# The second block's second product by a seven-product scheme, in passes of 768 tokens

## The chip, the cores and the metric

One core of one Trainium2 chip runs the whole program. The metric is the device time of one execution in microseconds. Before the change it is 907.19 us, the median of 3 runs (907.12 to 916.56).

## The reference, cut to what matters

```
attn_out = local band attention + upsampled attention on 4-token means   # q, k, v: 4 x 8 x 576 x 64
x  = attn_out as 2304 tokens x 512
h1 = x @ w_in        # 512 -> 2048
g1 = h1 * (1 / (1 + exp(-1.702 * h1)))
y  = g1 @ w_out      # 2048 -> 512
h2 = y @ w_in2       # second block, same sizes
g2 = maximum(0.01 * h2, h2)
out = g2 @ w_out2    # the product that the change recasts
```

The weights arrive as float64 bits; 512 KB hold one 128x512 tile of them.

## The kernel before

Everything is kept transposed: features lie on the 128 partitions, tokens along the columns. Each matrix product is made of three TensorE products, since every operand is split into a high part (rounded to the fp32r format) and a low part (the rest): low by high, high by low, high by high. One matmul has a 128x128 weight tile and a moving tile of up to 512 token columns.

A block is cut into token passes (`TB1` = 512, 448, 448, 448, 448 for the first block, `TB2` = 512, 512, 512, 512, 256 for the second). A unit is one pass j with one of 16 slices m of the 2048 hidden features: `l1_part` (line 723) makes 12 matmuls into an h bank (4 slices kc of 128 input features, 3 products each), `gate` (line 740) makes the activation and its two parts (ScalarE, VectorE, ScalarE, GpSimd: lines 753 or 760, 754 or 761, 151, 765), and `l2` (line 770) makes 12 matmuls into four output banks that collect over all 16 m. `l2` runs two units behind `l1_part` (`LAG` = 2). After the last m the four banks are scaled and stored, for the first block to the DRAM tensors `yd`, for the second to the output (lines 787 to 793).

Each engine works through its instructions in the order of the program text (`manual_schedule`, line 839). The attention and the first 14 units follow a list written out by hand (`ORDER`); from unit 14 on a loop (lines 853 to 873) runs `l1_part`, `gate`, the attention turns that are left, `l2`, and then weight work. All transfers are issued from SyncE's one queue.

The second block's weights are made while the first block runs. Between units 38 and 65 `w_next` (line 209) turns one float64 tile into float32 (`w_bits`, lines 160 to 183: one copy, three VectorE operations) and stores it to `wd`. During the first block's last pass `w_back` (line 226) reads both float32 tiles of an m back and splits them (ScalarE line 235, GpSimd line 236) into one of 16 weight slots of 8 KB per partition, in which they stay for the rest of the kernel.

Of the kernel before, what the change touches and what calls it, by code (L numbers as in the profile page):

```python
# [7 lines left out]
F32 = mybir.dt.float32  # L8
F32R = mybir.dt.float32r
# [7 lines left out]
P = 128  # L17
# [10 lines left out]
def attn_moe_kernel(ctx: ExitStack, tc, qT_d, kT_d, vh_d, vg_d, w1a, w2a, w1b, w2b, outT):  # L28
# [71 lines left out]
    ap = ctx.enter_context(tc.tile_pool(name="ap", bufs=1))  # L100
# [6 lines left out]
    wd = [dram.tile([P, 2, DM], F32, name=f"wd_{m}") for m in range(NM)]  # L107


    warm = const.tile([P, P], BF16, name="warm")  # L110
# [35 lines left out]
    def on(default):  # L146
        return chosen[0] or default
# [58 lines left out]
    pos = [0, 0]  # L206
    made = []

    def w_next():

        if made:
            m, i, t = made.pop()
            nc.sync.dma_start(out=wd[m][:, i], in_=t)
        while pos[0] < min(len(w_order), pos[1] + 3):
            w_load(1, *w_order[pos[0]])
            pos[0] += 1
        if pos[1] < len(w_order):
            m, i = w_order[pos[1]]
            t, fs = w_bits(1, m, i)
            run(fs)  # L220
            made.append((m, i, t))
        pos[1] += 1

    back = {}

    def w_back(m):

        while len(back) < min(NM, m + 3):
            n = len(back)
            back[n] = cv.tile([P, DM], I64, tag="stage", name=f"b_{n}", bufs=3).bitcast(F32)  # L230
            nc.sync.dma_start(out=back[n].rearrange("p (i n) -> p i n", n=DM), in_=wd[n])
        w_slot(1, m)
        t = back[m].rearrange("p (i n) -> p i n", n=DM)
        w = wt[1, m].rearrange("p (i k) n -> p i k n", k=2)
        nc.scalar.activation(out=w[:, :, 0].bitcast(F32R), in_=t, func=AF.Copy)  # L235
        nc.gpsimd.tensor_tensor(out=w[:, :, 1].bitcast(F32R), in0=t, in1=w[:, :, 0], op=ALU.subtract)  # L236

    ND, DS, DN = 3, 40, 48
# [437 lines left out]


    blk = []
    for e, tb in ((0, TB1), (1, TB2)):
        t0 = 0
        for n in tb:
            blk.append((e, t0, n))
            t0 += n
        assert t0 == NT
    units = [(j, m) for j in range(len(blk)) for m in range(NM)]
    NB1 = len(TB1)
    TM = max(TB1 + TB2)  # L690
    xs = {}

    def load_x(j, kc):
        e, t0, n = blk[j]
        t = mp.tile([P, TM], F32, tag="xf", name=f"xf_{j}_{kc}", bufs=KC)
        if e == 0:
            a = t0
            while a < t0 + n:
                b, o = divmod(a, S)
                w = min(S - o, t0 + n - a)  # L700
                nc.sync.dma_start(out=t[:, a - t0 : a - t0 + w], in_=xd[b][kc][:, o : o + w])
                assert jobs[NP * b + kc].done == S
                a += w
        else:
            nc.sync.dma_start(out=t[:, :n], in_=yd[kc][:, t0 : t0 + n])
        xf[j, kc] = t

    def split_hi(j, kc):
        n = blk[j][2]
        hi = mp.tile([P, TM], F32R, tag=f"xh{kc}", name=f"xh_{j}_{kc}")[:, :n]  # L710
        lo = mp.tile([P, TM], F32R, tag=f"xl{kc}", name=f"xl_{j}_{kc}")[:, :n]
        xs[kc] = (hi, lo)
        copy(hi, xf[j, kc][:, :n])

    def split_lo(j, kc):
        hi, lo = xs[kc]
        f = xf.pop((j, kc))[:, : blk[j][2]]
        on(V if j >= NB1 else XLO[kc]).tensor_tensor(out=lo, in0=f, in1=hi.bitcast(F32), op=ALU.subtract)  # L718

    gs = {}  # L720
    hs = {}

    def l1_part(u, kcs, bank=None):
        j, m = u
        w1h, w1l = wt[blk[j][0], m, 0]
# [6 lines left out]
        h = hs[u][:, : blk[j][2]]  # L732
        for kc in kcs:
            for i, (w, part) in enumerate(((w1l, 0), (w1h, 1), (w1h, 0))):
                nc.tensor.matmul(  # L735
                    h, w[:, kc * P : (kc + 1) * P], xs[kc][part],
                    start=kc == 0 and i == 0, stop=kc == KC - 1 and i == 2,
                )

    def gate(u):  # L740

        j, m = u
        n = blk[j][2]
# [6 lines left out]
        if blk[j][0] == 0:  # L750

            fs = [
                lambda: nc.scalar.activation(out=g, in_=h[:, :n], func=AF.Tanh, scale=0.5 * 1.702),  # L753
                lambda: nc.vector.scalar_tensor_tensor(  # L754
                    out=g, in0=g, scalar=1.0, in1=h[:, :n], op0=ALU.add, op1=ALU.mult
                ),
            ]
        else:
            fs = [
                lambda: nc.scalar.activation(out=g, in_=h[:, :n], func=AF.Copy, scale=0.01),  # L760
                lambda: nc.vector.tensor_tensor(out=g, in0=g, in1=h[:, :n], op=ALU.max),  # L761
            ]
# [6 lines left out]

    def l2(u):  # L770
        j, m = u
        e, t0, n = blk[j]
        gh, gl = gs.pop(u)
        w2h, w2l = wt[e, m, 1]
# [10 lines left out]
        scale = 0.5 if e == 0 else 1.0  # L785
        dst = yd if e == 0 else [outT[c * P : (c + 1) * P, :] for c in range(KC)]
        for c in range(KC):
            y = mp.tile([P, TM], F32, tag="xf", name=f"y_{j}_{c}", bufs=KC)[:, :n]
            if c % 2:
                nc.scalar.activation(out=y, in_=acc[c][:, :n], func=AF.Copy, scale=scale)  # L790
            else:
                nc.vector.tensor_scalar(out=y, in0=acc[c][:, :n], scalar1=scale, scalar2=None, op0=ALU.mult)
            nc.sync.dma_start(out=dst[c][:, t0 : t0 + n], in_=y)

    TURN, PERIOD = 2 * UNITS - 4, 6
    XL = NM - 4
# [42 lines left out]
    with tc.manual_schedule(engines={ET.PE, ET.DVE, ET.Pool, ET.Activation, ET.SP}):  # L839
# [10 lines left out]
            token(name)  # L850
        chosen[0] = None

        for u in range(UNITS, len(units) + LAG):
            if u < len(units):
                j, m = units[u]
                l1_part(units[u], range(KC))
                if m == NM - 1 and j + 1 < len(blk):
                    for kc in range(KC):
                        split_hi(j + 1, kc)
                        split_lo(j + 1, kc)  # L860
                run(gate(units[u]))
            run(turns.get(2 * u, []))
            if u >= LAG:
                l2(units[u - LAG])
                if units[u - LAG][0] == NB1 - 1:
                    w_back(units[u - LAG][1])
            while pos[1] < min(len(w_order) + 1, (u - AHEAD[0]) * len(w_order) // (AHEAD[1] - AHEAD[0])):
                w_next()
            run(turns.get(2 * u + 1, []))
            if u < len(units) and j + 1 < len(blk):  # L870
                for kc in range(KC):
                    if j > 1 and m == XL:
                        load_x(j + 1, kc)


# [47 lines left out]
```

## Time and profile before

| | us |
|---|---|
| median of 3 runs | 907.19 |
| the profiled execution's own time | 907.32 |
| its span, first to last instruction | 905.5 |
| PE busy in it | 895.1 |
| DVE, ACT, POOL busy | 405.7, 323.8, 337.7 |

PE is TensorE's matmuls, PEld its weight loads, DVE VectorE, ACT ScalarE, POOL GpSimd, SP SyncE (SPq its queue). Matmuls overlap one another, so the duration shown for one (0.39 us at 512 columns) is longer than the distance to the next; the rate is read from the starts, or from the pieces of the chain of waits, which gives a run of matmuls with its count. Attention and the first block's early units fill the first 300 us, the first block alone runs to about 503 us, the second block from there to the end.

### The profile page before, as it was taken

What the parts mean: (1) busy time and instruction counts of PE and PEld (TensorE: products, weight loads), DVE (VectorE), ACT (ScalarE), POOL (GpSimd) and SP (SyncE); (2) the same over time, 40 slices, a digit from 0 to 9 for tenths busy, and PEclk for the clock granted to TensorE, in tenths of its full rate; (3) what the DMA queues carried; (4) which work ended last, traced back from release to release, by engine and by line L of the source; (5) the groups of instructions that cost most, each with busy time, mean ns of one, the idle gap of its engine ahead of it and who ended that gap; (6) DMA issues with size and microseconds to landing.
All of it is one profiled execution on the core that took longest, in us unless ns stands there. A gap on an engine that the chain in (4) does not pass through costs nothing.

```text
span 905.5 us, 14436 instructions
## 1 busy us (share of the span) xinstructions
PE 895.1 (99%) x5681; PEld 764.4 (84%) x5681; DVE 405.7 (45%) x723; ACT 323.8 (36%) x713; POOL 337.7 (37%) x322
## 2 busy tenths in 40 slices
PE   8999999999999999999999999999999999999998
PEld 4687877888888899999999888888888888888898
DVE  7979997644455489888411311211121112111211
ACT  6865565322253123223344522322232223222322
POOL 5543535543554324224477622222222222222221
PEclk9999999999999999999999999999999999999999
DMA  8835543555444656666644300020002000200000
GB/s 279 273 111 157 187 163 108 167 151 144 152 131 133 204 177 224 230 198 227 195 136 142 132 1 1 1 93 1 1 1 93 1 1 1 70 0 1 29 20 24
DMA packets 51908, 98.70 MB, mean 109 GB/s; under 512 B 11648, under 2 KB 22912, under 8 KB 51840
## 3 DMA queue, kind: packets, MB, share of 16 engines
q1 hardware_dynamic: 51840, 97.77, 33.9%
q8 instruction: 45, 0.74, 0.3%
q14 instruction: 23, 0.19, 0.1%
HBM read 72.97 MB, written 24.77 MB: 108 GB/s over the span
## 4 chain that ended last, share of the span: by engine, by line
PE 96%; DVE 2%; ACT 1%; DMA 1%; issue 0%; SPq 0%; ACTq 0%
PE acc L780 44%; PE h L735 44%; PE av L568 2%; PE avd L509 2%; PE sc L351 1%; PE scd L434 1%; DMA a<-qT 1%; PE pt L528 0%; ACT a L407 0%; DVE a L325 0%; PE pdt L461 0%; DVE stat L402 0%; DVE stat_d L441 0%; DVE t L175 0%; DVE t L179 0%; DVE stat L398 0%
## 5 line engine op out<-in xcount | busy, mean ns | idle before, releaser
L780 PE MATMUL acc<-gh,w 128*128 128x512 f32 (+2 forms) x1280 | 393.5, 371 | 0.0
L735 PE MATMUL h<-xh,w 128*128 128x512 f32 (+2 forms) x1280 | 392.8, 370 | 0.0
L765 POOL TENSOR_TENSOR gl<-g,gh 128x512 fp32r<-128x512 f32 (+2 forms) x149 | 176.0, 1181 | 443.4 <-ACT gh L151 431.7
L780 PEld LDWEIGHTS acc<-gh,w 128*128 128x128 f32 x1280 | 237.3, 188 | 35.1 <-issue 2.0
L735 PEld LDWEIGHTS h<-xh,w 128*128 128x128 f32 x1280 | 237.3, 188 | 33.2
L735 PE MATMUL h<-xl,w 128*128 128x512 f32 (+2 forms) x640 | 236.2, 369 | 0.0
L780 PE MATMUL acc<-gl,w 128*128 128x512 f32 (+2 forms) x640 | 236.1, 369 | 0.0
L761 DVE TENSOR_TENSOR g<-g,h 128x512 f32<-128x512 f32 (+1 forms) x80 | 50.7, 634 | 315.5 <-ACT g L760 315.5
L151 ACT ACTIVATE gh<-g 128x512 fp32r<-128x512 f32 (+2 forms) x160 | 94.3, 590 | 123.5 <-DVE g L754 66.9
L735 PEld LDWEIGHTS h<-xl,w 128*128 128x128 f32 x640 | 120.5, 188 | 16.1
L780 PEld LDWEIGHTS acc<-gl,w 128*128 128x128 f32 x640 | 120.4, 188 | 15.7
L760 ACT ACTIVATE g<-h 128x512 f32<-128x512 f32 (+1 forms) x80 | 44.4, 555 | 220.9 <-PE h L735 220.6
L754 DVE SCALAR_TENSOR_TENSOR g<-g,h 128x448 f32<-128x448 f32 (+1 forms) x80 | 50.5, 632 | 122.9 <-ACT g L753 122.4
L753 ACT ACTIVATE g<-h 128x448 f32<-128x448 f32 (+1 forms) x80 | 44.3, 554 | 166.5 <-PE h L735 158.9
L175 DVE SCALAR_TENSOR_TENSOR t<-s,t 128x512 uint32<-128x512 uint32 x64 | 63.9, 1003 | 1.5
L198 POOL TENSOR_TENSOR w<-t,w 128x512 fp32r<-128x512 f32 x25 | 33.7, 1354 | 51.6 <-ACT w L151 46.5
L179 DVE SCALAR_TENSOR_TENSOR t<-s,t 128x512 uint32<-128x512 uint32 x64 | 45.6, 718 | 1.5
L236 POOL TENSOR_TENSOR w<-b,w 128x1024 fp32r<-128x1024 f32 x16 | 38.4, 2401 | 8.1 <-ACT w L235 8.1
L378 POOL TENSOR_TENSOR P<-P,stat 128x320 f32<-128x320 f32 (+1 forms) x37 | 30.0, 828 | 29.2 <-DVE stat L417 24.5
L172 DVE TENSOR_SCALAR t<-t 128x512 uint32<-128x512 uint32 x64 | 30.8, 484 | 3.5 <-ACT t L151 2.3
L718 DVE TENSOR_TENSOR xl<-xf,xh 128x512 fp32r<-128x512 f32 (+2 forms) x27 | 20.1, 760 | 17.6 <-ACT xh L151 17.6
L151 ACT ACTIVATE xh<-xf 128x512 fp32r<-128x512 f32 (+2 forms) x40 | 23.3, 589 | 12.5 <-PE h L735 10.3
(97 smaller groups left out, 561.9 us busy)
## 6 DMA issues: line engine op xcount, KB each, us to landing
s<-w1a SPq DMA_DIRECT2D x16, 512.0 KB, 4.2
s<-w2a SPq DMA_DIRECT2D x16, 512.0 KB, 4.1
s<-w1b SPq DMA_DIRECT2D x16, 512.0 KB, 3.9
s<-w2b SPq DMA_DIRECT2D x16, 512.0 KB, 4.3
wd<-t SPq DMA_DIRECT2D x32, 256.0 KB, 2.5
b<-wd SPq DMA_DIRECT2D x16, 512.0 KB, 3.6
xf<-yd SPq DMA_DIRECT2D x16, 256.0 KB, 3.6
outT<-y SPq DMA_DIRECT2D x16, 256.0 KB, 2.2
```

The lines of the kernel that those rows point to most:

```text
L151: return nc.scalar.activation(out=out, in_=in_, func=AF.Copy, scale=scale)
L175: lambda: nc.vector.scalar_tensor_tensor(out=b, in0=bits[:, :, 1], scalar=0x80000000, in1=b, op0=ALU.bitwise_and, op1=ALU.bitwise_or,),
L179: lambda: nc.vector.scalar_tensor_tensor(out=b, in0=bits[:, :, 0], scalar=29, in1=b, op0=ALU.logical_shift_right, op1=ALU.bitwise_or,),
L198: lambda: on(G).tensor_tensor(out=lo, in0=t, in1=wt[e, m][:, 2 * i, :], op=ALU.subtract),
L236: nc.gpsimd.tensor_tensor(out=w[:, :, 1].bitcast(F32R), in0=t, in1=w[:, :, 0], op=ALU.subtract)
L735: nc.tensor.matmul(h, w[:, kc * P : (kc + 1) * P], xs[kc][part], start=kc == 0 and i == 0, stop=kc == KC - 1 and i == 2,)
L753: lambda: nc.scalar.activation(out=g, in_=h[:, :n], func=AF.Tanh, scale=0.5 * 1.702),
L754: lambda: nc.vector.scalar_tensor_tensor(out=g, in0=g, scalar=1.0, in1=h[:, :n], op0=ALU.add, op1=ALU.mult),
L760: lambda: nc.scalar.activation(out=g, in_=h[:, :n], func=AF.Copy, scale=0.01),
L761: lambda: nc.vector.tensor_tensor(out=g, in0=g, in1=h[:, :n], op=ALU.max),
L765: lambda: on(G).tensor_tensor(out=gl, in0=g, in1=gh.bitcast(F32), op=ALU.subtract),
L780: nc.tensor.matmul(acc[c][:, :n], w[:, cs], g, start=m == 0 and i == 0, stop=m == NM - 1 and i == 2)
```

## The change

`TB2`, `w_next` and `w_back` go, and `gate` and `l2` serve the first block only. A class `Second` computes the second block in three passes p of 768 tokens, each two halves j of N2 = 384. Its first product is the same 12 matmuls per slice and half. Its second product is taken as a 2x2 by 2x2 block product: the 2048 hidden features in two halves k of 8 slices q, the 512 output features in two halves of 256, the tokens in two halves of 384. Seven block products of sums and differences take the place of eight. VectorE makes the sums on the activation side (four subtractions per q), the products go to four banks in two pairs, and the results are put together in SBUF as they are evicted.

Weights: during the first block (units 43 to 75, the list `prep`, spread evenly by weights noted in it, none in the unit with m = 14) the float64 tiles are converted with the copy on ScalarE, the four sums per q are made on VectorE, all is split, and the parts are stored to DRAM: `ws1` (16 x 512 KB) and `ws2` (8 x 1792 KB). In the second block nothing stays: per pass 16 tiles of `ws1` (512 KB) and 14 tiles of `ws2` (1 MB: four q of one product) are read, each two tiles ahead of use. The weight slots then hold 40 raw activations, a ring of five split operands, the `ws2` tiles and the next pass's input.

The order in the second block: 16 groups (p, q, k, j) of 12 matmuls fill the first chunk (four q); then each of six chunks takes 28 steps of 6 matmuls (7 products x 4 q), between which the 16 groups of the next chunk are laid; the last chunk has none. `prepare` makes the split operand three steps ahead.

```diff
-    TB2 = [512, 512, 512, 512, 256]
+    N2 = 384
+    NPAIR = NT // (2 * N2)
...
-    AHEAD = (38, 65)
+    PREP = (42, 75)
...
+    def prep_sums(q, k):
...
+        nc.vector.tensor_tensor(out=sm[:, k], in0=x, in1=y, op=op)
+    def split(hi, lo, t, e=None):
+        copy(hi.bitcast(F32R), t)
+        (e or G).tensor_tensor(out=lo.bitcast(F32R), in0=t, in1=hi, op=ALU.subtract)
...
+    def prep_store(q):
+        nc.sync.dma_start(out=ws2[q // QC][:, :, q % QC], in_=made.pop(("o", q)))
...
+    for q in range(NQD):
+        conv = [(w, lambda k=k: prep_conv(k)) for k, w in enumerate((0.3, 0.5, 1.0, 0.7))]
+        sums = [(0.4, lambda q=q, k=k: prep_sums(q, k)) for k in range(4)]
+        part = [(0.3, lambda q=q, k=k: prep_split(q, k)) for k in range(4)]
...
+        prep += conv + last + conv + sums + part[:2] + conv + low + part[2:] + conv[:3] + slow + store + conv[3:] + high
+        last = shigh
...
+    class Second:
...
+        SEQ = ((0, B11, 0, 0), (3, T1, 1, 0), (1, B21, 0, 1), (6, B22, 1, 1), (5, B12, 0, 0), (4, T2, 1, 0), (2, T4, 0, 1))
...
+        def first(self, p, q, k, j):
+            m = q + NQD * k
+            if j == 0:
+                self.load_w1()
...
+            pool, tag = ((ps_h, "h"), (ps_t, "t"))[self.n_h % 2]
...
+            for kc in range(KC):
+                hi, lo = self.x[p, j, kc]
+                ks = slice(kc * P, (kc + 1) * P)
+                for i, (a, x) in enumerate(((1, hi), (0, lo), (0, hi))):
+                    nc.tensor.matmul(
+                        h, w[:, a, ks], x, start=kc == 0 and i == 0, stop=kc == KC - 1 and i == 2
+                    )
+            g = self.free.pop(0)
+            nc.scalar.activation(out=g, in_=h, func=AF.Copy, scale=0.01)
+            nc.vector.tensor_tensor(out=g, in0=g, in1=h, op=ALU.max)
...
+            for o, a, b in ((t1, r[1], r[0]), (t2, r[3], t1), (r[1], r[3], r[1]), (t4, r[2], t2)):
+                nc.vector.tensor_tensor(out=o, in0=a, in1=b, op=ALU.subtract)
...
+        def prepare(self):
...
+            nc.scalar.activation(out=hi, in_=t, func=AF.Copy)
+            nc.gpsimd.tensor_tensor(out=lo, in0=t, in1=hi.bitcast(F32), op=ALU.subtract)
...
+        def products(self, ch, i, qs, cts):
...
+                    for k, (a, g) in enumerate(((1, hi), (0, lo), (0, hi))):
+                        nc.tensor.matmul(
+                            self.bank[pair, ct][:, :N2], w[:, q, a, cs], g,
...
+        def evict(self, ch, i, ct):
...
+            if c == 0 and i not in (4, 5):
+                nc.scalar.activation(out=y[name], in_=ps, func=AF.Copy)
+            else:
+                nc.vector.tensor_tensor(out=y[name], in0=ps, in1=y[name], op=ALU.add)
...
+            elif i == 5:
+                for n, half, j in (("e46", 1, 1), ("e7", 0, 1), ("e5", None, 0)):
+                    nc.vector.tensor_tensor(out=y[n], in0=y["u2"], in1=y[n], op=ALU.add)
...
+            elif i == 6:
+                store(y["e5"], 1, 0)
+        def second(self, s):
+            ch, i, q = self.steps[s]
+            if q == 0:
+                self.load_w2()
+            last = s >= len(self.steps) - QC
+            while self.n_prep < min(len(self.steps), s + 1 + (QC if last else self.LOOK)):
+                self.prepare()
...
+                for n in range(per):
+                    self.second(ch * per + n)
+                    while gs2 and len(gs2) > 16 - (n + 1) * 16 / 25:
+                        self.first(*gs2.pop(0))
...
+            if u > PREP[0] and m != NM - 2:
+                part = (u - PREP[0]) / (PREP[1] - PREP[0]) * sum(w for w, _ in prep)
+                while done < len(prep) and sum(w for w, _ in prep[: done + 1]) < part + 0.1:
+                    prep[done][1]()
```

## Rows read from the trace of the kernel before

**Rows 1.** The page, part 1: busy us, share of the span, instructions of each engine.

```profile
PE 895.1 (99%) x5681; PEld 764.4 (84%) x5681; DVE 405.7 (45%) x723; ACT 323.8 (36%) x713; POOL 337.7 (37%) x322
```

**Rows 2.** The page, part 4: chain that ended last, by engine.

```profile
PE 96%; DVE 2%; ACT 1%; DMA 1%; issue 0%; SPq 0%; ACTq 0%
```

**Rows 3.** Windows: us, engines' busy us, granted clock, DMA share, GB/s.

```profile
320.00:480.00 160.00, 160.00 (x791) 148.31 (x790) 108.72 (x156) 52.62 (x87) 66.53 (x48) 1.00 0.60 197
0.00:50.00 50.00, 43.51 (x569) 28.85 (x570) 42.10 (x99) 35.88 (x148) 28.14 (x38) 1.00 0.80 257
```

**Rows 4.** Chain of waits, pass of 512 columns: start us, us, what.

```profile
543.21 2.72 PE acc L780 x12
```

**Rows 5.** Chain of waits, pass of 448 columns, first and last of five pieces.

```profile
490.78 2.44 PE acc L780 x12
...
500.51 2.43 PE acc L780 x12
```

**Rows 6.** Chain of waits, last pass (256 columns) and end.

```profile
893.49 1.44 PE h L735 x12
...
897.81 4.33 PE acc L780 x36
...
902.16 0.38 ACT y L790
```

**Rows 7.** Timeline, the stores of the output at the end.

```profile
901.54 1.79 SPq L793 DMA_DIRECT2D outT<-y  x4
```

**Rows 8.** Groups by shape, second block (512 to 906 us): count, busy us, mean ns.

```profile
L761 DVE TENSOR_TENSOR g<-g,h 128x512 f32<-128x512 f32 x63 | 43.3, 687 | 272.4 <-ACT g L760 272.3
L718 DVE TENSOR_TENSOR xl<-xf,xh 128x512 fp32r<-128x512 f32 x12 | 8.2, 693 | 8.1 <-ACT xh L151 8.1
L761 DVE TENSOR_TENSOR g<-g,h 128x256 f32<-128x256 f32 x16 | 6.7, 421 | 40.6 <-ACT g L760 40.6
...
L718 DVE TENSOR_TENSOR xl<-xf,xh 128x256 fp32r<-128x256 f32 x4 | 1.7, 425 | 3.2 <-ACT xh L151 3.2
...
L765 POOL TENSOR_TENSOR gl<-g,gh 128x512 fp32r<-128x512 f32 x63 | 81.7, 1296 | 254.5 <-ACT gh L151 254.5
L765 POOL TENSOR_TENSOR gl<-g,gh 128x256 fp32r<-128x256 f32 x16 | 11.8, 736 | 36.7 <-ACT gh L151 33.2 <-PE acc L780 3.4
...
L151 ACT ACTIVATE gh<-g 128x512 fp32r<-128x512 f32 x63 | 39.9, 633 | 47.8 <-DVE g L761 47.8
...
L151 ACT ACTIVATE gh<-g 128x256 fp32r<-128x256 f32 x16 | 6.7, 417 | 7.8 <-DVE g L761 7.8
```

**Rows 9.** Groups by shape, first block alone (320 to 480 us).

```profile
L765 POOL TENSOR_TENSOR gl<-g,gh 128x448 fp32r<-128x448 f32 x33 | 38.4, 1164 | 87.9 <-ACT gh L151 80.2 <-PE acc L780 5.0 <-DMA wd<-t 2.7
L175 DVE SCALAR_TENSOR_TENSOR t<-s,t 128x512 uint32<-128x512 uint32 x29 | 38.2, 1316 | 1.0
...
L179 DVE SCALAR_TENSOR_TENSOR t<-s,t 128x512 uint32<-128x512 uint32 x30 | 20.8, 692 | 1.0
...
L172 DVE TENSOR_SCALAR t<-t 128x512 uint32<-128x512 uint32 x29 | 14.1, 485 | 1.0
```

**Rows 10.** Timeline, GpSimd and VectorE at once: start us, us, engine, instruction.

```profile
311.25 0.42 DVE L152 TENSOR_SCALAR t<-s 128x512 f32<-128x512 f32 x1
311.29 1.39 POOL L765 TENSOR_TENSOR gl<-g,gh 128x448 fp32r<-128x448 f32 x1 [4.81 <-ACT gh L151]
...
385.76 1.16 POOL L765 TENSOR_TENSOR gl<-g,gh 128x448 fp32r<-128x448 f32 x1 [3.71 <-ACT gh L151]
385.90 1.57 DVE L175 SCALAR_TENSOR_TENSOR t<-s,t 128x512 uint32<-128x512 uint32 x1
```

**Rows 11.** Timeline, one unit's gate, its first and last instruction.

```profile
481.15 0.55 ACT L753 ACTIVATE g<-h 128x448 f32<-128x448 f32 x1 [1.43 <-PE h L735]
...
483.04 1.16 POOL L765 TENSOR_TENSOR gl<-g,gh 128x448 fp32r<-128x448 f32 x1 [0.85 <-ACT gh L151]
```

**Rows 12.** The page, part 6: a read of split weights, KB, us to landing.

```profile
b<-wd SPq DMA_DIRECT2D x16, 512.0 KB, 3.6
```

More of the change, by code (lines that the diff above doesn't have):

```diff
@@ L106, in attn_moe_kernel @@
     yd = [dram.tile([P, NT], F32, name=f"yd_{c}") for c in range(KC)]
-    wd = [dram.tile([P, 2, DM], F32, name=f"wd_{m}") for m in range(NM)]
+    NQD = NM // 2
+    QC = 4
+    ws1 = [dram.tile([P, 2 * DM], F32, name=f"ws1_{m}") for m in range(NM)]
+    ws2 = [dram.tile([P, 7, QC, 2, DM // 2], F32, name=f"ws2_{c}") for c in range(NQD // QC)]
     warm = const.tile([P, P], BF16, name="warm")
@@ L205, in attn_moe_kernel @@
     w_order = [(m, i) for m in range(NM) for i in range(2)]
[L206 to L236, printed above, removed]
+    prep_order = [(m, i) for q in range(NQD) for i in (1, 0) for m in (q, q + NQD)]
@@ new lines, in attn_moe_kernel, with prep_conv @@
+    at = {"load": 0, "conv": 0}
+    made = {}
+    def prep_conv(k):
+        if k == 0:
+            while at["load"] < min(len(prep_order), at["conv"] + 3):
+                w_load(1, *prep_order[at["load"]])
+                at["load"] += 1
+            m, i = prep_order[at["conv"]]
+            at["conv"] += 1
+            made[m, i], made["fs"] = w_bits(1, m, i)
+            chosen[0] = nc.scalar
+        made["fs"][k]()
+        chosen[0] = None
+    def prep_sums(q, k):
+        H = DM // 2
+        t0, t1 = made[q, 1], made[q + NQD, 1]
+        if k == 0:
+            made["s", q] = rp.tile([P, 4, H], F32, tag="rs", name=f"sm_{q}")
+            made["o", q] = rp.tile([P, 7, 2, H], F32, tag="ra", name=f"wo_{q}")
+        sm = made["s", q]
+        x, y, op = (
+            (t0[:, H:], t1[:, H:], ALU.add),
+            (sm[:, 0], t0[:, :H], ALU.subtract),
+            (t0[:, :H], t0[:, H:], ALU.subtract),
+            (t1[:, :H], sm[:, 1], ALU.subtract),
+        )[k]
+        nc.vector.tensor_tensor(out=sm[:, k], in0=x, in1=y, op=op)
@@ new lines, in split, with prep_split @@
+    def split(hi, lo, t, e=None):
+        copy(hi.bitcast(F32R), t)
+        (e or G).tensor_tensor(out=lo.bitcast(F32R), in0=t, in1=hi, op=ALU.subtract)
+    def prep_split(q, k):
+        H = DM // 2
+        wo = made["o", q]
+        if k == 0:
+            split(wo[:, 0, 0], wo[:, 0, 1], made.pop((q, 1))[:, :H])
+        elif k == 1:
+            t = made.pop((q + NQD, 1)).rearrange("p (a n) -> p a n", n=H)
+            split(wo[:, 1:3, 0], wo[:, 1:3, 1], t)
+        else:
+            a = 2 * k - 4
+            split(wo[:, 3 + a : 5 + a, 0], wo[:, 3 + a : 5 + a, 1], made["s", q][:, a : a + 2])
@@ new lines, in prep_store, with prep_first, prep_store_first @@
+    def prep_store(q):
+        nc.sync.dma_start(out=ws2[q // QC][:, :, q % QC], in_=made.pop(("o", q)))
+    def prep_first(m):
+        t = made.pop((m, 0))
+        o = rp.tile([P, DM], F32, tag="rw", name=f"w1o_{m}", bufs=2)
+        split(o, t, t)
+        made["f", m] = (o, t)
+    def prep_store_first(m):
+        for i, t in enumerate(made.pop(("f", m))):
+            nc.sync.dma_start(out=ws1[m][:, i * DM : (i + 1) * DM], in_=t)
+    prep = []
+    last = []
+    for q in range(NQD):
+        conv = [(w, lambda k=k: prep_conv(k)) for k, w in enumerate((0.3, 0.5, 1.0, 0.7))]
+        sums = [(0.4, lambda q=q, k=k: prep_sums(q, k)) for k in range(4)]
+        part = [(0.3, lambda q=q, k=k: prep_split(q, k)) for k in range(4)]
+        low, high = [[(0.3, lambda m=m: prep_first(m))] for m in (q, q + NQD)]
+        slow, shigh = [[(0.0, lambda m=m: prep_store_first(m))] for m in (q, q + NQD)]
+        store = [(0.0, lambda q=q: prep_store(q))]
+        prep += conv + last + conv + sums + part[:2] + conv + low + part[2:] + conv[:3] + slow + store + conv[3:] + high
+        last = shigh
@@ L241, in attn_moe_kernel @@
+    prep += last
     ND, DS, DN = 3, 40, 48
@@ L681, in attn_moe_kernel @@
     blk = []
[L682 to L687, printed above, removed]
+    t0 = 0
+    for n in TB1:
+        blk.append((t0, n))
+        t0 += n
+    assert t0 == NT
     units = [(j, m) for j in range(len(blk)) for m in range(NM)]
-    NB1 = len(TB1)
-    TM = max(TB1 + TB2)
     xs = {}
     def load_x(j, kc):
-        e, t0, n = blk[j]
+        t0, n = blk[j]
         t = mp.tile([P, TM], F32, tag="xf", name=f"xf_{j}_{kc}", bufs=KC)
[L696 to L705, printed above, removed]
+        a = t0
+        while a < t0 + n:
+            b, o = divmod(a, S)
+            w = min(S - o, t0 + n - a)
+            nc.sync.dma_start(out=t[:, a - t0 : a - t0 + w], in_=xd[b][kc][:, o : o + w])
+            assert jobs[NP * b + kc].done == S
+            a += w
         xf[j, kc] = t
     def split_hi(j, kc):
-        n = blk[j][2]
+        n = blk[j][1]
         hi = mp.tile([P, TM], F32R, tag=f"xh{kc}", name=f"xh_{j}_{kc}")[:, :n]
@@ L795, in attn_moe_kernel @@
+    sec = Second()
     TURN, PERIOD = 2 * UNITS - 4, 6
@@ L851, in attn_moe_kernel @@
         chosen[0] = None
[L853 to L858, printed above, removed]
+        done = 0
+        rp = None
+        for u in range(UNITS, len(units)):
+            j, m = units[u]
+            l1_part(units[u], range(KC))
+            if m == NM - 1:
+                for kc in range(KC):
+                    if j + 1 < len(blk):
                         split_hi(j + 1, kc)
                         split_lo(j + 1, kc)
-                run(gate(units[u]))
+                    else:
+                        sec.split_x(0, 0, kc)
+            run(gate(units[u]))
             run(turns.get(2 * u, []))
[L863 to L868, printed above, removed]
+            l2(units[u - LAG])
+            if u > PREP[0] and m != NM - 2:
+                part = (u - PREP[0]) / (PREP[1] - PREP[0]) * sum(w for w, _ in prep)
+                while done < len(prep) and sum(w for w, _ in prep[: done + 1]) < part + 0.1:
+                    prep[done][1]()
+                    done += 1
             run(turns.get(2 * u + 1, []))
-            if u < len(units) and j + 1 < len(blk):
+            if u == PREP[0]:
+                ap_open.__exit__(None, None, None)
+                rp = ctx.enter_context(tc.tile_pool(name="rp", bufs=1))
+            if j + 1 < len(blk):
                 for kc in range(KC):
@@ L873, in attn_moe_kernel @@
                         load_x(j + 1, kc)
+            else:
+                if m == 2:
+                    for kc in range(KC):
+                        sec.load_raw(0, 1, kc)
+                if 6 <= m < 6 + KC:
+                    sec.split_x(0, 1, m - 6)
+                if m == 10:
+                    for kc in range(KC):
+                        sec.load_raw(0, 0, kc)
+                if m == 13:
+                    for _ in range(2):
+                        sec.load_w1()
+        assert done == len(prep)
+        sec.free = [x for k in range(8) for x in sec.cut(f"raw_{k}", F32)]
+        for _ in range(2):
+            sec.load_w2()
+        sec.main([lambda u=u: l2(units[u]) for u in range(len(units) - LAG, len(units))])
 def kernel(q, k, v, moe_w_in, moe_w_out, moe2_w_in, moe2_w_out):
```

193 lines of the change are left out of this document (168 added, 25 removed).

## The prediction

> **What bounds the kernel now.** I read the busy shares first: PE is busy for 895.1 of 905.5 us, no other engine for half of the span [rows 1]. Busy time alone proves nothing for overlapping matmuls, so the chain of waits comes next: 96% of it is PE, and neither a queue nor "issue" has a share [rows 2]. In the second block the chain is an unbroken row of pieces of 12 matmuls. What counts is the distance between starts: 2.72 us for 12 at 512 columns, 226.7 ns each [rows 4]; 1.44 us at 256 columns, 120.0 ns each [rows 6]; and from 490.78 to 500.51 us four pieces at 448 columns, 2.43 us each, 202.7 ns a matmul [rows 5]. Two units of any stretch cost the same, so no wait reaches PE there. The granted clock is 1.00 (2.4 GHz) throughout, also where the DMA engines are busy at 0.60 and 0.80 [rows 3]. PE's work is the time; the question is what the change takes from it and whether the new side work stays hidden.
>
> **PE's work.** In the second block there are 4 passes x 16 units x 24 = 1536 matmuls of 512 columns and 384 of 256. At the distances above that is 348.2 + 46.1 = 394.2 us. After the change the first product has 6 halves x 16 slices x 12 = 1152 matmuls of 384 columns, the second 3 passes x 7 products x 8 q x 2 output tiles x 3 = 1008, together 2160 (eight products would make 2304). No row has 384 columns in fp32r. It lies midway between 256 and 512, whose distances fit one line: (120.0 + 226.7) / 2 = 173.3 ns. The other end is the row at 448 columns: at 2.4 GHz these take 186.7 ns, the row shows 202.7, so 16.0 on top, against 13.3 at 256 and 512; with 16.0, 384 columns cost 176.0 ns. I take 173.3, since two rows that enclose 384 agree on it. 2160 x 173.3 = 374.4 us: **19.8 us less**. With 176.0 it is 380.2 us, 14.1 less. So the eighth saved of one product is partly paid back by 240 more matmuls of fixed cost.
>
> The Trainium skill (TensorE: Matmul & The Clock Gate, "Wait — 56ns, not 53.3ns?") puts the distance at N / 2.4 GHz plus about 2.5 ns. By that, an estimate, the block would go from 373.4 to 351.0 us, a gain of 22.4. It was measured in bf16; the fp32r rows here show 13.3 on top, and they decide.
>
> **Side work in the second block.** One chunk has 28 steps x 6 and 16 groups x 12 matmuls, (168 + 192) x 173.3 ns = 62.4 us of PE. Prices at 384 columns, midway between the rows at 256 and 512: VectorE from PSUM 554 ns, from SBUF 559, GpSimd 1016, ScalarE 525 [rows 8]. GpSimd: 28 low parts, 28.4 us. ScalarE: 16 + 28 copies, at most 10 evictions and 8 input splits, 32.6 us. VectorE: 16 maxima, 16 sums, 14 additions at eviction, 8 input splits, 30.0 us. Each is about half of 62.4, and there are four h banks in place of two, three steps of lead (3.1 us, 5 or more with the groups between) for a split that takes 0.53 + 1.02 us, and at least four steps between the eviction of a pair of banks and its next use. I cost it at nothing; PE's 62.4 us per chunk are the cover. The cover is thinnest in the last chunk, which has no groups: a step takes PE 1.04 us and GpSimd 1.02. Four of its 28 operands are made ahead, so GpSimd has 24.4 us of work in 24.9. It holds, and if each step took GpSimd 0.1 us more, the 2.4 us of lateness would be met by the ring's lead of four steps less one split, 4.16 - 1.55 = 2.6 us.
>
> Transfers there: 48 weight tiles of 512 KB, 42 of 1 MB, 4.7 MB in and 4.7 out, 78.6 MB in 374 us, 210 GB/s; in the last chunk 1 MB per 4.16 us, 252 GB/s. The opening 50 us moved 257 at a share of 0.80 [rows 3]. A 512 KB read lands in 3.6 us [rows 12]; a 1 MB read, with no row, in between that and twice it, 7.2 us, while two tiles of lead are 8.3 us in the last chunk and 19 elsewhere. On SyncE's queue a tile load waits for the buffer that PE frees just before, and an output store for VectorE's addition; behind such a store stand only loads that still have a tile's time. No cost, 3 us as upper end.
>
> **The first block's side work.** PE's work before 503 us is unchanged. The preparation moves from units 38 to 65 and the last pass into units 43 to 75: 33 units x 24 x 202.7 ns = 160.5 us. What hides it is the lag of two units: from the end of `l1_part` to the same unit's `l2` lie four pieces of 2.43 us, 9.7 us, and the gate needs 481.15 to 484.20, 3.1 us [rows 11]. So 6.6 us of lateness are free.
>
> Two resources come near their limit. First GpSimd and VectorE together, which hinder each other: with the GpSimd operation begun at 385.76 us, VectorE's next one lasted 1.57 us in place of 0.69, ending 0.55 after GpSimd's; with VectorE's begun at 311.25, GpSimd's lasted 1.39 in place of 1.16, ending 1.01 after [rows 9, 10]. They take turns, and only about 0.15 us of each operation lies outside its turn. GpSimd after the change: 33 gates x 1.164, 8 x (0.736 + 3 x 1.296) of splits, 16 x 1.296, 6 input splits x 1.164, 103 us. VectorE: 64 x 0.692 and 32 x 0.485 of conversion, 32 sums of 256 columns x 0.425, and 3.6 of input splits, 77 us. Laid end to end, 180 us; less 0.15 for each of the 221 operations, 147 us, 92% of 160.5. Second the DMA engines: 16.8 MB of float64, 8.4 + 14.7 MB of stores, 5.2 MB of x and y, 45.1 MB, 281 GB/s. Rows 3 give 328 (197 / 0.60) or 321 (257 / 0.80) at a share of 1, so 0.86 to 0.88. Both fit, but with cross-waits between queues: a split on ScalarE waits for VectorE's sums, and the next gate is queued behind it; a copy there waits for a float64 tile, which can stand behind a 1.8 MB store, 5.6 us at 325 GB/s. The unit with m = 14 gives no preparation and the next twice as much. I take **1 us** of stalls, between 0 and 8, near 0 because 6.6 us of slack take such bursts one by one. Dropping `w_back` (GpSimd and ScalarE, hidden) gains nothing.
>
> **The end.** Before, the last eviction ends 0.4 us after PE's last matmul [rows 6] and the stores follow [rows 7]. After, the evictions of product i = 5 put 8 additions on VectorE, 4.5 us, beside 4.16 us of PE; then two more of 0.55 come, 5.6 us, so the last ends 1.4 us after PE: **1 us more**, between 0.3 and 1.3 (192 KB to store for 128).
>
> **Sum.** Profiled execution 907.3 - 19.8 + 1 + 1 = **889.5 us**; that execution lies 0.1 us above the median, which changes nothing.
>
> **The rivals.** *A matmul of 384 columns costs 16.0 ns on top.* For it: the row at 448; against it: 256 and 512 agree on 13.3. Then 907.3 - 14.1 + 2 = 895 us.
>
> *GpSimd and VectorE become the bound of units 43 to 75.* If the turns were whole operations, 180 us stand against 160.5, 20 late; 6.6 are absorbed, so 13 to 20 us of PE stalls in place of 1: 902 to 908 us, no gain. For it: the 1.57 us of rows 10. Against it: the overlap of 0.15 in the same rows, 147 us; it decides only if waits between the queues leave the pair unused for over 8% of the time. The Trainium skill (SBUF — State Buffer, "Who interferes with whom") has this as a rule: a VectorE operation with two SBUF inputs, or in a two-port mode, and a GpSimd operation that reads SBUF exclude each other for the whole instruction. That they exclude each other the trace shows; for the whole of it, it does not.
>
> *The DMA engines become the bound there: slower.* If the queue, with 2 KB rows written to DRAM between the reads, could give no more than the 197 GB/s that the weight preparation moves now [rows 3] in place of 281, 45.1 MB would need 229 us, 68 late and 6.6 of it absorbed, some 950 us. It is slower by 1% once it delivers under about 240 (188 us for the stretch). For it: no row shows 281. Against it: 257 in the opening at a share of 0.80, and 197 at only 0.60.
>
> That it makes fewer products than eight is read from the loops, so I give no chance to the change not being what it says.
>
> **Chances and range.** A measurement here tells 1% (898.1 to 916.3 is no change). Forecast 0.58, near 889.5, with its bounds 886.5 to 894. 384 columns dearer, 0.12: 895. The pair as bound, 0.14: mostly no change, 0.02 of it below 898. DMA as bound, 0.09: slower. Left over 0.07, several late transfers or operands in the last chunks, 892 to 898, 0.01 of it slower. Faster 0.58 + 0.12 + 0.02 + 0.06 = 0.78, same 0.12, slower 0.10. The range 886.5 to 899 holds the forecast, the dearer matmul and the leftovers, about 0.78: its low end is the forecast without stalls and with the least tail and another 1 us of PE's distance, its high end the stalls of 8 us with half the dearer distance.
>
> **What would show it.** Matmuls of 384 columns 173.3 ns apart (the first step), 12 in 2.08 us; 2160 of them. PE's pieces of 2.43 us unbroken between 330 and 490 us, with VectorE's conversions longer than 0.69 us beside GpSimd's low parts (the preparation). A share of DMA below 0.9 there. After PE's last matmul some 1.4 us of VectorE. It would be wrong if PE shows gaps on GpSimd's low part in the last chunk, or on a weight tile.

## The result: no gain, 24 us lost before the second block begins

| | us |
|---|---|
| before, median of 20 runs | 907.56 |
| changed kernel, median of 20 runs | 914.84 (lowest 912.66) |
| ratio, 95% interval | 1.0085 (1.0065 to 1.0105) |
| forecast | 889.5, range 886.5 to 899 |

The profiled execution of the changed kernel took 923.17 us, span 921.4; unlike most of the 20 (by its time and mean clock only the one of 923.80 is like it) it runs 20 us of the opening at a granted clock of 0.50 (1.2 GHz), which costs 9.0 us (a run of first-block matmuls that starts at 156.69 us before starts at 165.68 here) and is taken off below.

The page of the changed kernel, parts 1 and 4 (beside [rows 1, 2]; the chain in part 4 reaches back to 416 us only, so its shares add up to some 54%):

```profile
PE 894.1 (97%) x5921; PEld 814.0 (88%) x5921; DVE 536.9 (58%) x901; ACT 383.8 (42%) x905; POOL 455.2 (49%) x442
...
PE 41%; DVE 7%; DMA 2%; ACT 2%; issue 2%; SPq 0%; DVEq 0%; ACTq 0%
```

The chain of waits, 96% PE before, now passes through DVE, ACT and DMA. Where it does so, the windows show (us, busy us of PE, PEld, DVE, ACT, POOL, granted clock, DMA share, GB/s):

```profile
40.00:60.00 20.00, 20.00 (x164) 16.20 (x161) 7.97 (x23) 7.83 (x31) 9.53 (x9) 0.50 0.37 103
...
355.00:535.00 180.00, 165.37 (x771) 146.97 (x770) 129.36 (x161) 82.09 (x155) 108.21 (x83) 0.97 0.70 241
549.00:914.00 365.00, 363.86 (x2098) 363.27 (x2097) 174.43 (x269) 137.63 (x307) 183.52 (x168) 1.00 0.56 200
```

From 549 us on PE is full. From 355 to 535 us, in the weight preparation, it is not, although no other engine is busy for more than 72% there. The chain gives the size of the loss (start us, us, what):

```profile
531.11 2.48 PE h L776 x12
533.59 2.48 PE acc L814 x12
536.07 4.17 PE h L908 x24
```

The second block's first product starts at 536.07, where the kernel before had it at 502.94 [rows 5, the piece after the last]: 33.1 us later, 9.0 of it from the opening, **24.1 us from the preparation**. Below, "lateness" is this figure for each kernel, read from its trace in the same way, at the last matmul of 448 columns before the second block and less what the opening gave; a further wait as the second block begins is not in it.

Not all of the 24.1 us are waits. Counted from start to start of the matmuls, 16.5 us lie at eleven gaps (PE's idle time in them is 14.6), 4.4 us in some 10 us at a granted clock of 0.50, 1.2 GHz (442.3 to 449.1 and 524.2 to 527.7 us, each beginning inside or between such gaps; matmuls of 448 columns start some 370 ns apart there, for 203), and 3.3 us in the slower rhythm of the last section.

From the second block's start to PE's last matmul at 917.1 us it is 381 us: the forecast's 374.4, 5.0 for the two `l2` of the first block that follow, and some 1.5, nearly all of it at one late weight tile.

### The profile page after: what moved, and what is told of

Its sections match the earlier page's. It is cut to its first block, busy times and chain, and to the rows that moved or that the text cites. A ratio compares the mean times of both kernels' runs of the same rounds, so it can differ in the third digit from the quotient of the medians.

```text
span 921.4 us, 15797 instructions
## 1 busy us (share of the span) xinstructions
PE 894.1 (97%) x5921; PEld 814.0 (88%) x5921; DVE 536.9 (58%) x901; ACT 383.8 (42%) x905; POOL 455.2 (49%) x442
## 4 chain that ended last, share of the span: by engine, by line
PE 41%; DVE 7%; DMA 2%; ACT 2%; issue 2%; SPq 0%; DVEq 0%; ACTq 0%
PE h L908 21%; PE p L955 18%; DVE t L181 2%; DVE t L185 1%; DVE t L178 1%; PE acc L814 1%; DVE sm L243 1%; DMA v<-ws 1%; DVE g L793 1%; ACT t L157 1%; PE h L776 1%; DMA s<-w1b 1%; ACT wo L157 1%; DMA s<-w2b 0%; DVE y L987 0%
## 5 line engine op out<-in xcount | busy, mean ns | idle before, releaser
L934 POOL TENSOR_TENSOR ring<-raw,ring 128x384 fp32r<-128x384 f32 x168 | 183.7, 1114 | 193.4 <-ACT ring L933 193.1
L776 PE MATMUL h<-xh,w 128*128 128x448 f32 (+1 forms) x640 | 203.7, 380 | 9.3 <-DVE g L793 8.8
L814 PE MATMUL acc<-gh,w 128*128 128x448 f32 (+1 forms) x640 | 201.8, 377 | 3.3 <-ACT gh L157 3.3
L955 PE MATMUL p<-ring,v 128*128 128x384 f32 x1008 | 188.0, 334 | 0.0
L955 PEld LDWEIGHTS p<-ring,v 128*128 128x128 f32 x1008 | 175.8, 188 | 0.3 <-POOL ring L934 0.3
L799 POOL TENSOR_TENSOR gl<-g,gh 128x448 fp32r<-128x448 f32 (+1 forms) x69 | 87.3, 1265 | 130.2 <-ACT gh L157 127.9
L776 PEld LDWEIGHTS h<-xh,w 128*128 128x128 f32 x640 | 122.2, 191 | 26.7 <-DVE g L793 11.7
L814 PEld LDWEIGHTS acc<-gh,w 128*128 128x128 f32 x640 | 121.0, 189 | 19.8 <-ACT gh L157 4.0
L776 PE MATMUL h<-xl,w 128*128 128x448 f32 (+1 forms) x320 | 120.7, 377 | 1.9 <-POOL xl L759 1.9
L814 PE MATMUL acc<-gl,w 128*128 128x448 f32 (+1 forms) x320 | 119.3, 373 | 0.1
L792 ACT ACTIVATE g<-h 128x448 f32<-128x448 f32 (+1 forms) x80 | 44.0, 549 | 116.8 <-PE h L776 98.5
```

Source lines behind the costliest of these rows:

```text
L776: nc.tensor.matmul(h, w[:, kc * P : (kc + 1) * P], xs[kc][part], start=kc == 0 and i == 0, stop=kc == KC - 1 and i == 2,)
L814: nc.tensor.matmul(acc[c][:, :n], w[:, cs], g, start=m == 0 and i == 0, stop=m == NM - 1 and i == 2)
L934: nc.gpsimd.tensor_tensor(out=lo, in0=t, in1=hi.bitcast(F32), op=ALU.subtract)
L955: nc.tensor.matmul(self.bank[pair, ct][:, :N2], w[:, q, a, cs], g, start=not more and q == 0 and k == 0, stop=q == QC - 1 and k == 2, skip ...
```

## What PE waited for

The views of waits of the changed kernel for 355 to 535 us, for PE, ACT and DVE (who waited for whom: us in total, times, longest):

```profile
PE h L776 <- DVE g L793: 8.8, 6, 2.4
PE acc L814 <- ACT gh L157: 3.3, 2, 2.1
PE h L776 <- POOL xl L759: 1.9, 2, 1.4
...
ACT w1o L157 <- DVE t L185: 32.8, 13, 4.6
ACT g L792 <- POOL gl L799: 11.0, 11, 1.5
...
DVE t L178 <- ACT t L157: 29.7, 20, 2.8
```

PE's largest wait is for an h bank that VectorE, in `gate`, has not read yet. ScalarE waits 33 us for VectorE's conversions before the high copy of a first-product tile (`w1o`, `prep_first`), and VectorE 30 us for ScalarE's conversion copy (`t`). One of PE's gaps in the timeline (start us, us, engine, instruction; in brackets the idle time before it and what ended that):

```profile
489.83 0.69 DVE L185 SCALAR_TENSOR_TENSOR t<-s,t 128x512 uint32<-128x512 uint32 x1
...
490.56 0.63 ACT L157 ACTIVATE w1o<-t 128x512 fp32r<-128x512 f32 x1 [2.44 <-DVE t L185]
...
491.10 1.14 ACT L157 ACTIVATE wo<-sm 128x512 fp32r<-128x512 f32 x2
...
492.14 0.51 ACT L891 ACTIVATE x3h<-x2f 128x384 fp32r<-128x384 f32 x1
...
492.40 0.37 PE L814 MATMUL acc<-gh,w 128*128 128x448 f32 x1
492.55 0.52 ACT L792 ACTIVATE g<-h 128x448 f32<-128x448 f32 x1
492.58 2.81 POOL L247 TENSOR_TENSOR wo<-sm,wo 128x512 fp32r<-128x512 f32 x2
...
492.68 1.58 DVE L892 TENSOR_TENSOR x3l<-x2f,x3h 128x384 fp32r<-128x384 f32 x1 [2.16 <-ACT x3h L891]
494.18 0.61 DVE L793 SCALAR_TENSOR_TENSOR g<-g,h 128x448 f32<-128x448 f32 x1
...
494.84 0.47 PE L776 MATMUL h<-xh,w 128*128 128x448 f32 x1 [2.08 <-DVE g L793]
```

Read it from below. PE, done with `l2` at 492.8, waits 2.08 us for a bank, which VectorE frees at 494.79. Until then VectorE was in an input split that took 1.58 us beside GpSimd's low parts (0.56 was the forecast's price for this size). The tanh (L792), which VectorE's operation needs, began only at 492.55: three weight copies and the copy of an input split stood ahead of it in ScalarE's queue, and before the first of these ScalarE had been idle for 2.44 us until VectorE's conversion was through. No single operation here is long; each queue waits for the other.

## The experiments

All were run beside the kernel before; the ratios are to it. Theory P: VectorE and GpSimd hinder each other and are together too slow. Theory Q: the in-order queues of ScalarE and VectorE wait for one another, and the gate stands behind. Theory D: the float64 tiles come late. Theory H (the double share of work behind the pause at m = 14) and theory G (one buffer for g) came up on the way.

**The copy on VectorE.**
```diff
-            chosen[0] = nc.scalar
+            chosen[0] = V
```


> The first copy of each weight conversion goes back from ScalarE to VectorE (32 copies of about 0.43 us); all else as in the changed kernel, which takes 914.8 us with some 24 us of PE stalls between 355 and 536 us. Theory Q (queue coupling: the copy on ScalarE stands behind split copies that wait for VectorE, VectorE's conversion then waits for that copy, and the next gate stands behind both): stalls fall to 10 us or less, 898 to 902 us. Theory P (VectorE and GpSimd take turns and are together too slow): 14 us more work for the pair, stalls grow, 920 to 930 us. Theory D (float64 tiles land late): 914 us, unchanged.


909.35 us, ratio 1.0019 (0.9996 to 1.0041), lateness 19.6, between what Q and P expected. VectorE no longer waits for ScalarE, but its copy, 0.42 us alone in the kernel before [rows 10], now lasts 0.8 (first row below, from the groups of this kernel by shape, 345 to 525 us), and the pair is loaded more (VectorE or GpSimd busy for 96% of 345 to 520 us, for 91% of 355 to 535 in the changed kernel). The other half of Q stayed: ScalarE waits for VectorE before `w1o` as long as before (32.0 us for 32.8, row below under "at once").

```profile
L158 DVE TENSOR_SCALAR t<-s 128x512 f32<-128x512 f32 x29 | 23.7, 817 | 1.7 <-POOL wo L247 1.7
L178 DVE TENSOR_SCALAR t<-t 128x512 uint32<-128x512 uint32 x29 | 22.6, 779 | 0.9
```

**The low parts on ScalarE.**
```diff
-        (e or G).tensor_tensor(out=lo.bitcast(F32R), in0=t, in1=hi, op=ALU.subtract)
+        nc.scalar.activation(out=lo.bitcast(F32R), in_=t, func=AF.Copy)
```


> In the preparation the low part of each weight is a second copy on ScalarE in place of the subtraction on GpSimd (this leaves out the subtraction, so the stored low parts are not the low parts). GpSimd loses 48 operations, about 58 us in the preparation; ScalarE gets 48 copies, about 28 us. Theory P: the pair has 40 per cent less to do and the stalls go, 890 to 894 us. Theory Q: ScalarE's queue is longer and still waits for VectorE, 912 to 925 us. Theory D: 914 us.


906.65 us, 0.9985 (0.9963 to 1.0007), lateness 17.9. GpSimd is out of the preparation of the weights, and three quarters of the loss remain: P alone falls.

**Half the float64 reads.**
```diff
...
+        if e == 1 and m >= NM // 2:
+            stage[e, m, i] = twin.pop((m - NM // 2, i))
+            return
...
+        if e == 1:
+            twin[m, i] = s
```


> Every second float64 tile of the second block is not read; its conversion takes the tile read before (this leaves out half of those reads, 8.4 MB of 45 MB in the preparation, so half of the weights are wrong). The conversions themselves are unchanged. Theory D: the stalls fall by half or more, 898 to 904 us. Theories P and Q: within 3 us of the changed kernel, 911 to 916 us.


913.95 us, 1.0062 (1.0039 to 1.0084), lateness 24.0; the DMA share in the stretch falls from 0.70 to 0.60, and the loss stays. D falls.

**No pause at m = 14.**
```diff
-            if u > PREP[0] and m != NM - 2:
+            if u > PREP[0]:
```


> The unit with m = 14 gets its share of preparation too, so the unit with m = 15 no longer gets a double share. Theory H (the double share behind the pause is what uses up the lag): stalls fall from 24 to about 12 us, 901 to 905 us. Theories P, Q, D: the total is the same, 910 to 917 us, with later input splits at the pass boundaries.


911.27 us, 1.0040 (1.0011 to 1.0069), lateness 19.3 (in a profiled run that was 3.0 us below its median). Both effects showed: PE's waits for `gate` behind the double share shrink, those for the next pass's input split (`xl`) grow from 1.9 to 6.2 us. H explains a few us, not the loss.

**Splits held back by one unit** (the list of split copies and stores is issued after the next unit's gate; four kernels: alone; with the copy on VectorE; with that and the low parts on ScalarE; and with the copy on VectorE over 35 units in place of 33).
```diff
...
+            if kind in ("late", "free", "store"):
+                held.append((f, kind))
+                return
...
             run(gate(units[u]))
+            flush()
...
```


> Same instructions as the changed kernel; only their order in the preparation differs: the split copies and the stores of one unit are issued after the next unit's gate, when the conversions that they wait for are done. The changed kernel has 24 us of PE stalls before its second block. Theory Q (the next gate stands in ScalarE's queue behind a split copy that waits for VectorE's conversion): stalls fall below 12 us, about 902 us. Theory P (GpSimd and VectorE in turns are too slow in total): nothing changes, 911 to 916 us.

> As the kernel with the splits held back by one unit, and the first copy of the conversion on VectorE, so that neither engine waits for the other inside a unit (with the copy alone moved, 909.4 us and 19.6 us of stalls). Theory Q: stalls of 5 us or less, 893 to 897 us. Theory P: 14 us more for the pair than in the changed kernel, no better than 909 us.

> As the kernel with held splits and the copy on VectorE, and the low parts made by a second ScalarE copy in place of GpSimd's subtraction (this leaves out the subtraction). Neither the pair nor the cross-waits are left. Theories P and Q together: no stalls beyond 2 us, 890 to 893 us. If there is a third cause (late float64 tiles, the double share behind the pause at m = 14), stalls stay above 6 us, 897 us or more.

> As the kernel with held splits and the copy on VectorE, but the preparation is spread over units 43 to 77 in place of 43 to 75, 6 per cent more time. Theory P (capacity): stalls fall by about 8 us against the same kernel over 33 units. Theory Q: by 2 us or less.


935.76, 931.06, 903.19 and 945.00 us (ratios 1.0314, 1.0264, 0.9957, 1.0391), lateness 37.6, 35.3, 10.7 and 34.1, and a further wait of 2 to 12 us as the second block starts. Q had expected the first below 12 us and the second at 5 or less; both went the other way, so the reading of Q behind this edit was too simple. The conversion tiles `t` have three buffers; held longer, they were missing for the next conversion, which then waited for a store or a split. From the waits of the first of these, for ACT:

```profile
ACT t L157 <- DMA ws<-t: 26.7, 7, 8.7
...
ACT t L157 <- POOL wo L247: 9.0, 6, 2.2
```

So these four bring in a wait of their own and decide neither for nor against Q; they show that the split must also not come late.

**A second buffer for g.**
```diff
-        o = rp.tile([P, DM], F32, tag="rw", name=f"w1o_{m}", bufs=2)
+        o = rp.tile([P, DM], F32, tag="rw", name=f"w1o_{m}", bufs=1)
...
-        g = mp.tile([P, TM], F32, tag="g", name=f"g_{nm}")[:, :n]
+        g = mp.tile([P, TM], F32, tag="g", name=f"g_{nm}", bufs=2)[:, :n]
...
```


> The activation tile g gets a second buffer (its 2 KB come from the tile of the split first weights, which goes from two to one). Theory G (with one g buffer the next tanh waits until GpSimd has read g for the low part, which stands behind the preparation in GpSimd's queue, so the lag of two units cannot be used): stalls fall from 24 us to 10 or less, about 900 us. Theories P and Q (work and waits of the preparation itself): 910 to 916 us.


913.40 us, 1.0064 (1.0049 to 1.0079), lateness 23.8. The tanh's waits for GpSimd (`g`, 11.0 us) are gone, and the loss is not: G falls, though a wait of 3.7 us before `w1o`, which has one buffer less, is new.

**Copy on VectorE and low parts on ScalarE at once** (the two edits above together).


> Both single edits at once: the first copy of the conversion on VectorE, the low parts of the preparation as a second ScalarE copy (this leaves out the subtraction). Order as in the changed kernel. Alone they took 5.5 and 8 us off 914.8. If the two causes are separate: 901 us. If both only relieve one and the same queue: 905 to 907 us. If the order of the splits is right as it is and only the load of the pair counts: below 897 us.


893.63 us, 0.9849 (0.9834 to 0.9864), lateness 3.8. Alone the two took 4.5 and 6.2 us off the lateness, together 20.3. This is the range that the expectation gave to "only the load of the pair counts", but the load doesn't explain it: with only the low parts moved to ScalarE, VectorE or GpSimd is busy for 69% of 345 to 520 us, and 17.9 us are lost; here it is 81% of 345 to 505 us, and 3.8 are lost. What falls is ScalarE's wait before `w1o`, first with the copy on VectorE, then with the low parts on ScalarE, then with both:

```profile
ACT w1o L157 <- DVE t L185: 32.0, 13, 4.4
...
ACT w1o L157 <- DVE t L185: 21.0, 12, 2.5
...
ACT w1o L157 <- DVE t L185: 15.4, 10, 2.5
```

So P and Q hang together: without GpSimd's low parts beside them VectorE's three conversion operations are shorter (with only the low parts moved, 2.16 us a tile in place of 2.88), and ScalarE waits less for them. Each single edit leaves 18 to 20 us; both together leave little, though this kernel is not wholly without Q.

**The first product's weights split in the second block.**
```diff
...
-        split(o, t, t)
-        made["f", m] = (o, t)
+        made["f", m] = made.pop((m, 0))
...
+        def split_w1(self):
+            if self.n_s1 < len(self.w1_seq):
+                t = self.w1[self.w1_seq[self.n_s1]]
+                nc.scalar.activation(out=t[:, 0].bitcast(F32R), in_=t[:, 1], func=AF.Copy)
+                nc.gpsimd.tensor_tensor(out=t[:, 1].bitcast(F32R), in0=t[:, 1], in1=t[:, 0], op=ALU.subtract)
...
```


> The first product's weights are stored unsplit (256 KB in place of 512 KB per tile) and split in the second block, one tile ahead of use, 48 times in place of 16. The preparation loses 16 ScalarE copies, 16 GpSimd subtractions (20.7 us) and 4.2 MB of stores; the second block gains 48 of each, about 62 us of GpSimd beside 379 us of PE. ScalarE's waits for the conversion before those copies (33 us in the changed kernel) go too. Theories P and Q: stalls fall from 24 to 8 to 14 us, 899 to 905 us; second block unchanged. If the second block's GpSimd becomes late: no gain, 912 us or more.

> As the kernel that splits the first weights in the second block, and the first copy of the conversion on VectorE. Theory Q (ScalarE's waits): better than without the copy moved by 3 us or more, 895 to 900 us. Theory P (the pair): worse than without it by 2 to 5 us.


895.66 us, 0.9869 (0.9854 to 0.9884), and, with the copy on VectorE as well, 896.49, 0.9878 (0.9861 to 0.9894); lateness 3.4 and 3.5. Better than expected, and where the copy stands no longer matters, which neither theory had expected.

**Which half of that split?** Its GpSimd subtraction, or its ScalarE copy:
```diff
-        split(o, t, t)
+        copy(o.bitcast(F32R), t)
```


> As the changed kernel, but the 16 tiles of the first product's weights get their high copy on ScalarE only; the 16 subtractions on GpSimd (1.3 us each, 20.7 us) are left out and the unsplit tile is stored as the low part. ScalarE's order and all stores are the same. Theory P (GpSimd and VectorE in turns): most of what splitting these weights later won comes from here, stalls fall from 24 to about 10 us, 898 to 903 us. Theory Q (ScalarE's copies wait for VectorE's conversion, the next gate behind them): no more than 4 us, 910 us or more.


904.52 us, 0.9955 (0.9930 to 0.9981), lateness 13.8, between the two expectations. ScalarE's wait before `w1o` stays (31.2 us), so the 10.3 us won here come from GpSimd's work.
```diff
-        split(o, t, t)
-        made["f", m] = (o, t)
+        G.tensor_tensor(out=o.bitcast(F32R), in0=t, in1=t, op=ALU.subtract)
+        made["f", m] = (t, o)
```


> The complement: the 16 subtractions on GpSimd stay, the 16 high copies on ScalarE, which wait for the conversion, are left out (the unsplit tile is stored as the high part, zeros as the low part). Theory Q: stalls fall from 24 to about 10 us, 898 to 903 us. Theory P: 910 us or more.


896.09 us, 0.9865 (0.9816 to 0.9914), lateness 7.3. Sixteen copies of 0.63 us, 10 us of ScalarE's time, are worth 16.8 us of PE (12.4 at the gaps, counted as above, and 4.4 of half clock, which this kernel does not have in the stretch); 20.7 us of GpSimd's are worth 10.3. Of these splits Q was the larger part. ScalarE's waits in this kernel, without the copies: the row for `w1o` is gone, and a longer wait of the gate for GpSimd (25.0 against 11.0 us) costs PE little.

```profile
ACT gh L157 <- DVE g L793: 54.1, 33, 5.3
ACT g L792 <- POOL gl L799: 25.0, 18, 3.6
```

**The better kernel.** The kernel that splits the first weights later still waited 2.3 us at its second block's start, by its waits of PE:

```profile
PE h L915 <- POOL v L867: 2.3, 1, 2.3
```
The edit, against that kernel:
```diff
-                if m == 13:
+                if m == 12:
...
-                if m == 15:
+                if m == 14:
                     sec.split_w1()
```


> As the kernel that splits the first product's weights in the second block, with the first tiles loaded at m = 12 and the first one split at m = 14 of the last pass in place of m = 13 and 15. That kernel waits 2.7 us at the start of the second block and runs some 1.7 us more there at half the clock. If that wait is the late split: 891.5 us. If it is something else (the input split, a late tile): 895.7 us, unchanged.


**889.14 us, ratio 0.9785 (0.9743 to 0.9828)**, lateness 0.6. Its page, part 1, and its window from 335 to 525 us:

```profile
PE 875.4 (99%) x5921; PEld 804.1 (91%) x5921; DVE 568.0 (64%) x901; ACT 398.9 (45%) x937; POOL 503.7 (57%) x474
```
```profile
335.00:525.00 190.00, 189.68 (x950) 176.68 (x950) 137.28 (x182) 87.55 (x167) 101.24 (x78) 1.00 0.65 226
```

PE is full, with VectorE as busy as in the slow kernel (72%). It beats both kernels, and lands where the forecast had put the change, but only with those sixteen splits out of the preparation. Not all of the 6.5 us against the kernel that it builds on come from the edit: 4.2 were expected, and nearly 3 lie, by the two profiled runs, in the rhythm of the last section, most of it in a stretch in which the two programs are the same.

## Why the prediction was wrong

**PE's work: right.** The groups of twelve are 2.08 us, 173.3 ns a matmul. The rival with 16.0 ns on top falls. From the chain of waits of the changed kernel:

```profile
575.36 2.08 PE h L908 x12
578.48 2.08 PE h L908 x12
580.56 2.08 PE p L955 x12
```

**Side work in the second block: right but for one tile.** GpSimd's low parts took 1114 ns on the mean for 1016, VectorE's sums 873 for 559 where both read SBUF, and PE waited for neither:

```profile
L934 POOL TENSOR_TENSOR ring<-raw,ring 128x384 fp32r<-128x384 f32 x168 | 183.7, 1114 | 193.4 <-ACT ring L933 193.1
...
L920 DVE TENSOR_TENSOR raw<-raw,raw 128x384 f32<-128x384 f32 x74 | 62.1, 873 | 1.8
```

PE waited once, 1.3 us before 715.86, for a weight tile that took 8.83 us to land; SyncE's queue had issued its load behind input loads that waited for a buffer. 3 us had been the upper end:

```profile
706.89 8.83 DMA v<-ws
715.73 0.14 issue
715.86 2.34 PE h L908 x12
```

**The end: right.** The forecast was 1.4 us from PE's last matmul to the last eviction; it went from 917.1 to 918.5.

**The first block's side work: wrong, and this is nearly the whole error.** The step that takes 1 us of stalls, "near 0 because 6.6 us of slack take such bursts one by one", measured 24.1, outside its own bounds of 0 to 8. I had named the pieces ("a split on ScalarE waits for VectorE's sums, and the next gate is queued behind it") and then priced only resources: the pair 92% busy, the DMA engines 0.87. The pair's share came out, 91% of 355 to 535 us with VectorE or GpSimd busy; but in the better kernel, whose PE is full, it is 93% of 345 to 501 us, so this share alone does not tell whether PE waits. Two things failed.

The wait was not in the sum: ScalarE is idle before 13 of the copies, 2.5 us on the mean, 33 us in all, in a queue that the sum does not price in these units at all, and that is busy for only 82 of the 180 us. The experiments that take the sixteen splits apart show the ScalarE copies with this wait as the larger cause (16.8 us) and GpSimd's subtractions as the smaller (10.3).

And the slack is not granted anew at each unit. The timelines tell how long after the last matmul of its h bank each tanh starts: 0.1 us in most units of the kernel before, 2.6 to 9.6 us in every unit from 48 to 77 of the changed kernel, 0.1 to 3.7 us in the better kernel. PE sets the pace, so a unit whose gate starts late hands its lateness on until the queue before the gate has less than a unit's work; the tanh at 492.55 was 7.2 us behind, a unit and a half. The forecast also took the slack at `l2` only. With two h banks, the `l1_part` after the next one needs the bank read after three pieces, 7.3 us, and there PE waited most, 8.8 us of 14.6. What the stalls cost on top, the half clock, had no term either.

**The rivals.** The pair as bound (902 to 908 us, 13 to 20 us of stalls) had the place and about the size, but as sole mechanism it is refuted: without GpSimd 17.9 us remain. That the two hinder each other was confirmed: L181 and L185 last 976 and 974 ns on the mean, for 0.69 us alone [rows 9, 10], and L178, with one SBUF input, 928 ns for 485 before [rows 9]. But part of this was there before: L175, which is L181 now, took 1316 ns [rows 9], so the three together grew only from 2.49 to 2.88 us a tile. The Trainium skill (SBUF — State Buffer, "Who interferes with whom") states the exclusion as a rule, for two SBUF inputs or a two-port mode. The trace agrees for L181 and L185, less the 0.15 us of overlap in [rows 10]; in which mode L178 ran no run here shows. The DMA rival falls: 241 GB/s at a share of 0.70, and with 8.4 of some 45 MB not read the same time. The kernel came out at 914.84, inside what I called no change, at a chance of 0.12.

## What to carry to other kernels

Work that is moved under a full engine must be costed by the queues' order as well as by their load: for each instruction ask what it waits for, and what then stands behind it. Here sixteen copies of 0.6 us, most of which waited 2.5 us in the queue of the critical gate, cost 1.7 times their own time. Slack between a stage and its consumer is a stock that is used up over many units and refilled only where the queue has room to catch up, not a grant for each. When two limits hold at once, taking one away shows little; take both away before a theory is dropped, and look in the trace whether the edit took away the wait that it was meant to.

## What was not expected of the hardware

At 448 columns two rhythms occur. Before, twelve matmuls take 2.43 us [rows 5]; in the changed kernel they take 2.48 us for long stretches between gaps (the rows at 531.11 and 533.59 above), 206.7 ns each for 202.7, at the granted clock of 1.00. Behind a gap either can follow and then holds. The kernel that splits the first weights later and the better one built on it have the same program up to the last pass's unit with m = 12, and PE has one gap of 0.3 us in the same place; behind it the first runs at 2.48 until the second block, the second at 2.43 (first two rows below, one of each chain):

```profile
362.02 2.48 PE h L772 x12
...
361.49 2.43 PE h L772 x12
...
506.72 2.48 PE acc L810 x12
```

In the first kernel this alone is about 3 of its 3.4 us. The last row is again the better kernel: the slower rhythm also comes without a gap, behind 24 matmuls of 384 columns. What sets the rhythm stays open.
